# A delta-rule attention and hash-routed experts kernel: TensorE products placed by a count of work, and the first three groups loaded by 192 KB

## The chip, the core and the metric

The kernel runs on one core of one Trainium2 chip. The metric is the device time of one launch in microseconds (us). The five engines are named as in the profile: PE is TensorE, ACT is ScalarE, DVE is VectorE, POOL is GpSimd, SP is SyncE. PE's clock has two levels, 2.4 GHz (granted clock 1.00) and 1.2 GHz (0.50); the profile's rows give the granted clock of a stretch. PE writes its products to eight banks of PSUM, and ACT and DVE copy them from there.

## What is computed

Stage one is a delta rule over 4 batches, 8 heads, 768 positions and a head size of 48; stage two sends each of the 3072 rows through one of eight experts, which a hash of its token chooses.

```python
for t in range(768):
    y[:, :, t] = einsum('bhd,bhde->bhe', q[:, :, t], state)
    v_old = einsum('bhde,bhd->bhe', state, k_n[:, :, t])      # k_n = k / |k|
    state = state + beta_t * einsum('bhd,bhe->bhde', k_n[:, :, t], v[:, :, t] - v_old)
x = y.transpose(0, 2, 1, 3).reshape(3072, 384)
expert = token_ids * 2654435761 % 8
for e in range(8):
    out[expert == e] = maximum(x[expert == e] @ w1[e], 0) @ w2[e]
```

All arithmetic is in f32.

## The kernel before

Stage one cuts the sequence into 24 chunks of 32 positions. Four chunks form a group, so there are six groups.

For each group, work that doesn't depend on the state goes ahead of the chunks:

- K, Q and V come by 48 KB loads on SP's queue, four for each chunk and tensor (`load`, line 400). A load puts the 32 positions of one batch on 32 partitions, in runs of 192 bytes.
- `turn` (line 433) transposes the four 128x128 blocks of a chunk's K or Q on PE, and ACT copies the result to a tile KQ.
- `gram` (line 460) makes the products of keys with keys and of keys with queries, 128 small ones for two chunks (K and Q together), and ACT copies them to GK and GQ. `first_grams` (line 496) does it for the keys of group 0.
- `inverse` runs on DVE. It transposes GK to NT (line 547), works out scales, and then takes 31 steps, each a multiplication (line 582) and a subtraction (line 580) that need the one before. `turn_back` (line 594) transposes the result to TU. Two inverses can be under way at a time, since their tiles exist twice.

Each chunk then has a chain, in which every step needs the one before: `ask` (line 617, keys with the state, to psX), a subtraction on DVE (line 640, to R), `solve` (line 650, to psX; it needs the tile Tz, which ACT makes of TU), a copy on ACT (line 668, to W), `update` (line 677, to psS) and the copies to the next state (lines 701 and 699). The answers (line 721) and the queries' `ask` fill psY, ACT copies that to x_sb, and POOL scatters it to x_scratch (line 733).

No engine picks its own order. Each piece is a `task` with an estimated duration, and `order()` plays the whole stage with these estimates, engine by engine, and always takes the ready task with the longest way to the end. The instructions are then issued in the order that this play gives, and each engine runs its own in that order.

`order()` also places products whose result nobody reads, `unread` (line 602): a 128x128 identity against up to 512 columns. Before the first `update` they fill planned idle time of PE, with their target in a spare bank. After it, `chunk` itself adds one task with four blocks of 128 columns (`REST`; two blocks from chunk 20 on) behind each `update`, and drops it where a transposition or gram is ready. The play knows one speed of PE.

Stage two begins when the last rows have been scattered. It fetches an expert's rows (`fetch`, xr), transposes them on DVE, and runs two matrix products for each expert (lines 1103 and 1133), with the scatter of the results on POOL. The change doesn't touch it.

## Time and profile before

| | us |
|---|---|
| median of 3 runs (532.03 to 533.23) | 532.6 |
| the profiled execution | 535.72 |
| its span, first to last instruction | 534.1 |

| engine | busy us | share of the span |
|---|---|---|
| PE | 472.0 | 88% |
| DVE | 249.5 | 47% |
| ACT | 159.5 | 30% |
| POOL | 136.7 | 26% |

The shares are means over two stages that differ. The profile's slices show DVE nearly full for the first half of the span and nearly idle later, while PE is full in the second half. The slices also give PE's clock: it is below full in most of the slices of the first half, and full in the second. The chain that ended last, as the page prints it, holds only the last microsecond (a scatter on POOL), so the stages have to be read from rows of stretches.

### The profile page before, as it was taken

What the parts mean: (1) busy time and instruction counts of PE and PEld (TensorE: products, weight loads), DVE (VectorE), ACT (ScalarE), POOL (GpSimd) and SP (SyncE); (2) the same over time, 40 slices, a digit from 0 to 9 for tenths busy, and PEclk for the clock granted to TensorE, in tenths of its full rate; (3) what the DMA queues carried; (4) which work ended last, traced back from release to release, by engine and by line L of the source; (5) the groups of instructions that cost most, each with busy time, mean ns of one, the idle gap of its engine ahead of it and who ended that gap; (6) DMA issues with size and microseconds to landing.
All of it is one profiled execution on the core that took longest, in us unless ns stands there. A gap on an engine that the chain in (4) does not pass through costs nothing. (4 is left out here: it accounts for less than half of the span.)

```text
span 534.1 us, 15767 instructions
## 1 busy us (share of the span) xinstructions
PE 472.0 (88%) x6640; PEld 330.8 (62%) x6640; DVE 249.5 (47%) x735; ACT 159.5 (30%) x339; POOL 136.7 (26%) x166
## 2 busy tenths in 40 slices
PE   7787967898999997988199999999999999999991
PEld 5555655677677765766146657666675766767650
DVE  6584787867978989897022113121121212112100
ACT  2325655556856855664000010000101000010100
POOL 5000000302312112111100171452706244260731
PEclk9759979668969978999789999999999999999997
DMA  4455454546543312252696550905417072000101
GB/s 86 76 88 88 82 88 86 111 103 156 105 83 67 75 49 50 58 203 106 111 306 241 134 191 9 301 29 159 166 35 276 16 227 98 7 35 1 39 18 28
DMA packets 108280, 55.93 MB, mean 105 GB/s; under 512 B 95620, under 2 KB 104269, under 8 KB 107312
## 3 DMA queue, kind: packets, MB, share of 16 engines
q1 hardware_dynamic: 102688, 45.15, 34.9%
q0 software_dynamic: 5472, 9.65, 5.1%
q8 instruction: 53, 0.87, 0.7%
q14 instruction: 19, 0.16, 0.1%
q10 hardware_dynamic: 48, 0.10, 0.0%
HBM read 44.51 MB, written 10.62 MB: 103 GB/s over the span
## 5 line engine op out<-in xcount | busy, mean ns | idle before, releaser
L1103 PE MATMUL h_ps<-xT,w_sb 128*128 128x424 f32 (+3 forms) x384 | 128.8, 495 | 12.1 <-DMA xr<-x_scratch 12.1
L1140 POOL DMA_INDIRECT out_dram<-o_sb,idx x90 | 88.3, 981 | 161.3 <-DVE o_sb L1135 89.6
L1103 PEld LDWEIGHTS h_ps<-xT,w_sb 128*128 128x128 f32 x384 | 73.5, 192 | 65.3 <-issue 28.1
L1133 PE MATMUL o_ps<-h_sb,w_sb 128*128 128x424 f32 (+3 forms) x336 | 112.3, 494 | 0.0
L1133 PEld LDWEIGHTS o_ps<-h_sb,w_sb 128*128 128x128 f32 x336 | 84.4, 251 | 27.2 <-issue 0.3
L1106 ACT ACTIVATE h_sb<-h_ps 128x424 f32<-128x424 f32 (+3 forms) x32 | 15.9, 497 | 232.7 <-PE h_ps L1103 211.2
L1108 DVE TENSOR_SCALAR h_sb<-h_ps 128x424 f32<-128x424 f32 (+3 forms) x32 | 18.1, 565 | 112.5 <-PE h_ps L1103 89.7
L733 POOL DMA_INDIRECT x_scratch<-x_sb,slot x24 | 24.6, 1026 | 160.9 <-ACT x_sb L727 59.6
L580 DVE TENSOR_TENSOR U<-U,tmp 128x31 f32<-128x31 f32 (+15 forms) x186 | 61.3, 338 | 2.4
L582 DVE TENSOR_TENSOR tmp<-U,NT 128x175 f32<-128x175 f32 (+15 forms) x186 | 60.7, 336 | 2.5
L1135 DVE STREAM_TRANSPOSE o_sb<-o_ps 128x384 f32<-128x384 f32 (+2 forms) x21 | 15.6, 743 | 79.4 <-PE o_ps L1133 79.4
L701 ACT ACTIVATE S<-psS 48x384 f32<-48x384 f32 x86 | 41.8, 486 | 13.6 <-PE psS L677 8.8
L650 PE MATMUL psX<-R,Tz 64*64 64x48 f32 x736 | 32.3, 235 | 10.1 <-DVE R L640 8.3
L650 PEld LDWEIGHTS psX<-R,Tz 64*64 64x64 f32 x736 | 27.5, 147 | 16.5 <-DVE R L640 8.1
L721 PE MATMUL psY<-W,MT 64*64 64x48 f32 x768 | 33.7, 234 | 1.6 <-issue 1.6
L677 PE MATMUL psS<-W,K 32*128 32x96 f32 x736 | 32.1, 310 | 1.1 <-issue 0.8
L531 ACT ACTIVATE Tz<-TU,kmask 128x256 f32<-128x256 f32 x48 | 31.1, 728 | 0.9 <-DVE TU L594 0.7
L677 PEld LDWEIGHTS psS<-W,K 32*128 32x128 f32 x736 | 27.4, 209 | 4.6 <-ACT W L668 1.7
L617 PE MATMUL psX<-S,KQ 128*32 128x96 f32 x736 | 27.5, 275 | 3.0 <-ACT S L701 2.0
L617 PE MATMUL psY<-S,KQ 128*32 128x96 f32 x736 | 26.6, 277 | 3.3 <-ACT x_sb L727 2.1
L721 PEld LDWEIGHTS psY<-W,MT 64*64 64x64 f32 x768 | 28.6, 147 | 1.3 <-issue 1.1
L617 PEld LDWEIGHTS psY<-S,KQ 128*32 128x32 f32 x736 | 18.9, 124 | 12.1 <-ACT S L701 5.3
(144 smaller groups left out, 475.9 us busy)
## 6 DMA issues: line engine op xcount, KB each, us to landing
w_sb<-in_moe_w_dram SPq DMA_DIRECT2D x14, 1536.0 KB
K<-in_k_dram SPq DMA_DIRECT2D x96, 48.0 KB
Q<-in_q_dram SPq DMA_DIRECT2D x96, 48.0 KB
V<-in_v_dram SPq DMA_DIRECT2D x96, 48.0 KB
xr<-x_scratch SPq DMA_DIRECT2D x16, 145.5 KB
w_sb<-in_moe_w_dram SPq DMA_DIRECT2D x3, 512.0 KB
w_sb<-in_moe_w_dram SPq DMA_DIRECT2D x4, 384.0 KB
out_dram<-o_sb,idx POOLq DMA_INDIRECT x90
```

The source lines that it names most:

```text
L531: lambda e=e: nc.scalar.activation(out[:, :, :, e], in_, ACT.Copy, scale=kmask[:, e:e + 1]))
L580: nc.vector.tensor_tensor(U[:, n:, 0:n], U[:, n:, 0:n], t, op=ALU.subtract)
L582: nc.vector.tensor_tensor(t, U[:, j:n, 0:n].to_broadcast([P, m, n]), NT[:, j, n:, None].to_broadcast([P, m, n]), op=ALU.mult)
L617: nc.tensor.matmul(res[quarter(to), u], lhsT=KQ[:, u, a, quarter(b)], rhs=S0[:, b, u].rearrange("p r d -> p (r d)"), start=(fresh and u == ...
L650: nc.tensor.matmul(pws[i][rows, h], lhsT=Tz[rows, h].rearrange("p e i -> p (e i)"), rhs=R[rows, h], start=(h == hs.start), stop=True, skip ...
L677: nc.tensor.matmul(psS["all"][:, b, 2 * D * u:2 * D * u + 2 * D], lhsT=K[quarter(b), u].rearrange("p r d -> p (r d)"), rhs=W[quarter(b), 2 ...
L701: nc.scalar.activation(to, new, ACT.Copy)
L721: nc.tensor.matmul(py[to, h], lhsT=MT[rows, h].rearrange("p e i -> p (e i)"), rhs=W[rows, h], start=(c == 0 and h == 0), stop=True, skip_g ...
L733: put = nc.gpsimd.indirect_dma_start(out=x_dram[:, :], out_offset=bass.IndirectOffsetOnAxis(ap=slot[:, c:c + 1], axis=0), in_=x_sb.rearran ...
L1103: nc.tensor.matmul(h_ps[:, :width], lhsT=w1_sb[:, co, fo * P:(fo + 1) * P], rhs=xT[:, co, :width], start=(co == 0), stop=(co == CO - 1))
L1133: nc.tensor.matmul(os_ps[i][:, 0:width], lhsT=w2_sb[:, fo, i::CO], rhs=h_sb[:, fo, 0:width], start=(fo == 0), stop=(fo == FO - 1))
L1140: scat = nc.gpsimd.indirect_dma_start(out=out_q, out_offset=bass.IndirectOffsetOnAxis(ap=idx[e][:, k:k + 1], axis=0), in_=o_sb[:, k], in_o ...
```

## The change

1. The first three groups (0 to 2) get their K and Q by 192 KB loads, one for each batch, group and tensor: 128 positions on 128 partitions (`load_batches`). `turn_batches` transposes them, and the results go to three new tiles KQg that hold a group each. The 192 KB loads borrow the last four K tiles. `load` stays for the other groups, for V, and for the K that `update` reads. All K and Q of groups 0 to 2 are listed ahead of chunk 0, with all grams of groups 1 and 2.
2. `order()` now counts the work in PE's array. A task has an `area`, and `run` adds it up by spans of the constant `WINDOW` from a fixed start (`PHASE`). In the span after one with too little (`SHARE`) the play runs PE at half speed.
3. Products are placed by this play everywhere, not by `chunk`. They go into planned idle time, and where the sum lately is below `FORCE`, a whole one is placed even if nothing is idle. After the first `update` the target is psX0, the bank z0, or psS; to psS goes a product with zeros (`add_nothing`), which adds nothing to the state. `REST` and its task are gone.
4. The groups' priorities (`HASTE`), and the estimates of a load's issue and rate, are new numbers.

```diff
-        NK, NQ, NV, NKQ = 7, 2, 3, 14
-        HASTE, DRAG = 10000.0, 1.0
+        NK, NQ, NV, NKQ, NEAR = 7, 2, 3, 14, 3
+        TURNS = [(0, 0), (1, 0), (0, 1), (1, 1), (2, 0), (2, 1)]
+        HASTE = {(0, 3): 25000.0, (0, 4): 25000.0, (0, 5): 25000.0}
...
-        FILL_NS, AFTER, REST, EARLY = 215, 200, 4, 34
+        FILL_NS, AFTER, EARLY = 215, 200, 34
+        PHASE, WINDOW, SHARE, FORCE = 1200.0, 3413.33, 0.36, 0.40
...
+        KQgs = tiles(NEAR, "KQg", [P, GC, HU, 2, P])
+        KQs = [t[:, i] for t in KQgs for i in range(GC)]
+        KQs += tiles(NKQ - len(KQs), "KQ", [P, HU, 2, P])
...
+            def speed(w):
+                full = PHASE + w * WINDOW < 9000 or work.get(w - 1, 0.0) >= SHARE * WINDOW
+                return 1.0 if full else 0.5
...
+            def lately(t):
+
+                return sum(a * (e - max(b, t - WINDOW)) / (e - b) for b, e, a in runs[-24:]
+                           if e > t - WINDOW)
...
+                if e == "PE":
+
+                    idle = until
+                    while idle > 6000:
+                        k = speed(int((idle - PHASE) // WINDOW))
+                        m = min(BANK // P, int((s - AFTER - idle) * k // FILL_NS))
+                        if begun_state and lately(s) < FORCE * WINDOW:
+                            m = BANK // P
+                        z = banks[0] is not None and banks[0] <= idle
+                        to = 0 if not begun_state else 1 if open_x else 2 if z else 3 if (
+                            open_s is not None and open_s <= idle) else None
+                        if m < (1 if not begun_state else 2) or to is None:
+                            break
+                        m = min(m, 3) if to == 3 else m
+                        fills.append((idle + 1, -(m + 8 * to)))
+                        idle = run(idle, FILL_NS * m, 214.0 * m)
...
-                    while idle + FILL_NS + AFTER <= s and idle > 6000 and not begun_state:
-                        k = min(BANK // P, int((s - AFTER - idle) // FILL_NS))
-                        fills.append((idle + 1, -k))
...
+        def load_batches(g, a):
+            for b in range(B):
+                t, names = by_batch(g, a, b)
+                task("SP", 450, (), names, lambda t=t, b=b: nc.sync.dma_start(
+                    out=t.rearrange("p u r d -> p (u r) d")[:, :, 0:D],
+                    in_=(k_r, q_r)[a][b][GC * C * g:GC * C * g + GC * C]), kb=192)
...
+        def add_nothing(n):
+
+            nc.tensor.matmul(psS["all"][:, 0, 0:n * P].rearrange("p (x y) -> p x y", y=P),
+                             lhsT=nought, rhs=ident[:, None, :].to_broadcast([P, n, P]),
+                             start=False, stop=True, skip_group_check=True)
...
-                n = REST if c < SHARED else REST // 2
-                task("PE", 264 * n, ("psS",), ("psX0",),
-                     lambda: unread(psXs[0], n), words=4, kind="U", filler=True)
...
-            for p in range(4):
-                load_k(p)
-            for c in range(GC):
-                turn(c, 0)
+            load_batches(0, 0)
+            load_batches(1, 0)
+            turn_batches(0, 0)
...
+            load_batches(0, 1)
+            turn_batches(1, 0)
+            load_batches(1, 1)
+            turn_batches(0, 1)
             gram(range(GC), (1,))
+            load_batches(2, 0)
+            turn_batches(1, 1)
+            load_batches(2, 1)
...
```

What this moves is shown at three places. In the rows a matmul's target stands ahead of the arrow and its operands behind, with rows x columns; x8 is a count.

SP at the program's start, before:

```order
L400 DMA K0_75<-in_k_dram 32x8x48 x8
L400 DMA K1_76<-in_k_dram 32x8x48 x8
L400 DMA Q0_82<-in_q_dram 32x8x48 x4
L400 DMA Q1_83<-in_q_dram 32x8x48 x4
L400 DMA Q0_82<-in_q_dram 32x8x48 x4
```

and now (Q0 and Q1 are 48 KB loads for chunks 12 to 15):

```order
L460 DMA K3_78<-in_k_dram 128x8x48 x2
L460 DMA K4_79<-in_k_dram 128x8x48 x2
L460 DMA K5_80<-in_k_dram 128x8x48 x2
L460 DMA K6_81<-in_k_dram 128x8x48 x2
L447 DMA Q0_82<-in_q_dram 32x8x48 x6
L460 DMA K5_80<-in_q_dram 128x8x48
L447 DMA Q0_82<-in_q_dram 32x8x48
```

Sixteen 48 KB loads of the first keys became four of 192 KB, the keys of group 1 follow at once, and their queries come before those of group 0. Ahead of the last 192 KB load there are now 23 others and 24 loads of 48 KB.

PE from the last grams ahead of chunk 0 to chunk 1's first `ask`, before:

```order
L602 MATMUL spare3_150<-ident_59 128x512 x3
L602 MATMUL spare3_150<-ident_59 128x384
L650 MATMUL psX0_141<-V0_86,Tz0_116 64x48 x8
L650 MATMUL psX1_142<-V0_86,Tz0_116 64x48 x8
L677 MATMUL psS_1224<-W0_90,K0_75 128x96 x16
L433 MATMUL z0_140<-ident_59,K6_81 128x128 x4
L617 MATMUL psX0_141<-S1_85,KQ1_95 32x96 x8
```

and now:

```order
L689 MATMUL spare3_141<-ident_59 128x512 x2
L689 MATMUL spare3_141<-ident_59 128x384
L743 MATMUL psX0_132<-V0_86,Tz0_107 64x48 x8
L743 MATMUL psX1_133<-V0_86,Tz0_107 64x48 x8
L689 MATMUL spare3_141<-ident_59 128x512 x2
L689 MATMUL spare3_141<-ident_59 128x256
L770 MATMUL psS_1205<-W0_90,K0_75 128x96 x16
L689 MATMUL psX0_132<-ident_59 128x512
L710 MATMUL psX0_132<-S1_85,KQg0_94 32x96 x8
```

The transposition of K6 (a chunk of group 3) no longer stands ahead of chunk 1's `ask`; it comes behind chunk 3's `solve`. Products stand there instead. The transposition of K0 for chunk 14 now stands between the halves of chunk 1's `update`.

PE behind the `update` of chunk 15, before:

```order
L677 MATMUL psS_1224<-W1_91,K0_75 128x96 x16
L602 MATMUL psX0_141<-ident_59 128x512
L617 MATMUL psY_143<-S1_85,KQ1_95 32x96 x8
L617 MATMUL psX0_141<-S0_84,KQ2_96 32x96 x8
L617 MATMUL psY_143<-S1_85,KQ1_95 32x96 x8
L617 MATMUL psX1_142<-S0_84,KQ2_96 32x96 x8
```

and now:

```order
L770 MATMUL psS_1205<-W1_91,K0_75 128x96 x16
L710 MATMUL psY_134<-S1_85,KQg0_94 32x96 x16
L689 MATMUL z0_131<-ident_59 128x256
L710 MATMUL psX0_132<-S0_84,KQg0_94 32x96 x8
L689 MATMUL z0_131<-ident_59 128x256
L710 MATMUL psX1_133<-S0_84,KQg0_94 32x96 x8
```

One product of 512 columns became two of 256, and the queries' `ask` stands ahead of them. From chunk 1 on, the change has 49 blocks of 128 columns of unread products and 16 of zeros; before there were 58 blocks: a product of 512 columns ahead of the `ask` of chunks 4, 8 to 10 and 12 to 20, and one of 256 at chunks 21 to 23. Now chunks 5, 6, 8, 9, 10, 21 and 22 have none at all.

## Rows read from the trace of the kernel before

**Rows 1.** By stretch (start:end, length): busy us, instructions, PEclk, DMA share, GB/s

```profile
core 0: us, PE busy (x) PEld busy (x) DVE busy (x) ACT busy (x) POOL busy (x), PEclk, DMA share, GB/s
...
61.20:98.90 37.70, 29.45 (x664) 22.60 (x658) 29.19 (x102) 21.83 (x48) 2.47 (x4) 0.84 0.48 83
98.90:137.00 38.10, 34.06 (x833) 26.23 (x830) 28.80 (x104) 23.21 (x51) 8.06 (x13) 0.76 0.57 124
137.00:173.00 36.00, 33.64 (x947) 25.99 (x949) 30.57 (x96) 24.44 (x55) 7.22 (x10) 0.86 0.43 85
173.00:206.40 33.40, 30.68 (x975) 23.52 (x964) 29.75 (x92) 21.71 (x49) 6.50 (x10) 0.90 0.28 67
206.40:232.20 25.80, 22.53 (x632) 16.77 (x632) 22.77 (x70) 16.88 (x36) 5.40 (x8) 0.87 0.17 46
...
267.90:534.10 266.20, 254.25 (x768) 166.81 (x768) 48.04 (x85) 16.85 (x34) 93.31 (x93) 0.98 0.37 116
```

**Rows 2.** Timeline of DVE, 38 to 48 us: start, length, names, idle before

```profile
38.27 0.42 DVE L580 TENSOR_TENSOR U<-U,tmp 128x247 f32<-128x247 f32 x1
47.10 1.25 DVE L547 STREAM_TRANSPOSE NT<-GK 128x1024 f32<-128x1024 f32 x1 [8.42 <-ACT GK L471]
```

**Rows 3.** Timeline of SP's queue at the start: start, length, loads issued

```profile
0.94 7.83 SPq L400 DMA_DIRECT2D K<-in_k_dram  x16
8.82 9.88 SPq L400 DMA_DIRECT2D Q<-in_q_dram  x16
```

**Rows 4.** A stretch of 48 KB loads, columns as in rows 1

```profile
18.70:61.00 42.30, 34.83 (x832) 24.28 (x818) 31.09 (x106) 16.43 (x35) 0.00 (x0) 0.80 0.52 87
```

**Rows 5.** A stretch of the expert rows' loads (388-byte runs), columns as before

```profile
262.00:264.00 2.00, 0.00 (x0) 0.00 (x0) 0.00 (x0) 0.00 (x0) 0.00 (x0) 0.50 1.26 217
```

**Rows 6.** Timeline of PE at chunk 0

```profile
64.67 1.14 PE L650 MATMUL psX<-V,Tz 64*64 64x48 f32 x32
```

**Rows 7.** Timeline of PE behind chunk 0

```profile
65.77 1.17 PE L677 MATMUL psS<-W,K 32*128 32x96 f32 x32
70.67 1.09 PE L433 MATMUL z<-ident,K 128*128 128x128 f32 x4 [3.73 <-DMA K<-in_k_dram]
```

**Rows 8.** One stretch at the full clock, two at the lower, columns as before

```profile
90.00:93.40 3.40, 0.93 (x48) 0.81 (x51) 3.40 (x15) 0.65 (x2) 0.00 (x0) 0.99 0.56 100
93.40:103.60 10.20, 10.00 (x226) 7.43 (x217) 8.15 (x29) 5.25 (x11) 3.85 (x5) 0.50 0.53 115
107.00:117.30 10.30, 10.30 (x245) 8.72 (x248) 6.11 (x18) 5.87 (x14) 0.00 (x0) 0.50 0.51 100
```

**Rows 9.** Chunks 10, 12, 14, 17 and 18, update to update, columns as before

```profile
154.50:164.20 9.70, 9.70 (x233) 7.41 (x232) 5.96 (x22) 4.42 (x11) 0.00 (x0) 0.63 0.20 34
171.30:178.25 6.95, 6.48 (x179) 5.00 (x182) 6.67 (x17) 6.75 (x16) 2.18 (x3) 1.00 0.58 118
188.40:197.30 8.90, 8.90 (x227) 7.16 (x227) 6.87 (x24) 3.93 (x10) 0.00 (x0) 0.62 0.18 43
212.40:219.10 6.70, 6.70 (x163) 4.82 (x163) 4.44 (x12) 4.08 (x9) 1.35 (x2) 0.71 0.18 49
219.10:224.70 5.60, 5.13 (x164) 3.77 (x163) 5.39 (x15) 3.95 (x9) 1.19 (x2) 1.00 0.26 66
```

**Rows 10.** Groups of PE: line, names, shapes, count, busy us, mean ns

```profile
L602 PE MATMUL psX<-ident 128*128 128x512 f32 (+1 forms) x32 | 20.2, 712 | 0.4 <-issue 0.4
L460 PE MATMUL z<-KQ 48*32 48x64 f32 x768 | 19.8, 265 | 1.3 <-issue 1.2
...
L433 PE MATMUL z<-ident,K 128*128 128x128 f32 x60 | 10.6, 304 | 3.9 <-DMA K<-in_k_dram 3.7
```

More of the change, by code (lines that the diff above doesn't have):

```diff
@@ L257, in order @@
                 t = tasks[i]
-                rest[i] = t["ns"] * t["drag"] + max([t["more"]] + [lag(i, j) + rest[j] for j in after[i]])
+                rest[i] = t["ns"] + max([t["more"]] + [lag(i, j) + rest[j] for j in after[i]])
             chance = random.Random(SEED)
-            rest = [x + t["boost"] + chance.uniform(-SPREAD, SPREAD)
+            rest = [x + t["boost"] + HASTE.get(t["group"], 0.0) + chance.uniform(-SPREAD, SPREAD)
                     for x, t in zip(rest, tasks)]
@@ L321, in order @@
                 t = tasks[pick]
-                if t["filler"] and any(x <= at + 150 and tasks[i]["kind"] in "GT"
-                                       for x, i in r):
-                    t.update(ns=0, words=0, kind=kind, emit=lambda: None)
                 ready[e] = [p for p in ready[e] if p[1] != pick]
@@ L444, in keys_of @@
         def keys_of(c, parts=(0,)):
-            return tuple(f"KQ{c % NKQ}{a}" for a in parts)
+            return tuple(f"KQ{c % NKQ}{a}{b}" for a in parts for b in range(B))
         def gram(cs, parts=(0, 1)):
@@ L451, in gram @@
             cc, a0, a1 = slice(cs[0] % GC, cs[0] % GC + len(cs)), parts[0], parts[-1] + 1
+            held_keys = [x for c in cs for x in keys_of(c, sorted({0, *parts}))]
             def view(job):
@@ L951, in note @@
             turn_back(0)
[L952 to L958 removed]
+            load_batches(0, 1)
+            turn_batches(1, 0)
+            load_batches(1, 1)
+            turn_batches(0, 1)
+            gram(range(GC), (1,))
+            load_batches(2, 0)
+            turn_batches(1, 1)
+            load_batches(2, 1)
+            for c in range(GC, 2 * GC, 2):
+                gram((c, c + 1))
+            inverse(1)
+            turn_batches(2, 0)
+            turn_batches(2, 1)
+            for c in range(2 * GC, 3 * GC, 2):
+                gram((c, c + 1))
+            turn_back(1)
+            inverse(2)
+            for p in range(NV):
+                load_k(p)
+                load_v(p)
+            for p in range(NV, NK):
+                load_k(p)
             def prepare(p):
                 cs = range(2 * p, 2 * p + 2)
[L963 to L964 removed]
+                group[0] = (0, p // 2)
+                if p >= NK:
                     load_k(p)
```

129 lines of the change are left out of this document (81 added, 48 removed).

## Prediction

> **What bounds the kernel now.** I read the rows by stretch first. Stage two, from 267.9 us to the end, has PE busy 254.25 of 266.20 us at a clock of 0.98 [rows 1]. The change leaves it alone, so whatever is gained must move its start. Up to there a chain of 24 chunks runs beside six inverses on DVE. From the first TU (61.2) to the last (232.2), DVE is busy 29.19 + 28.80 + 30.57 + 29.75 + 22.77 = 141.1 of 171.0 us [rows 1]. Its work there stays, so these 171 us can give at most the 29.9 us in which DVE idles. PE is no less loaded, but part of its load is its own slowness: from the granted clocks, (1 - PEclk) x 2 x length sums to 12.1 + 18.3 + 10.1 + 6.7 + 6.7 = 53.9 us at the lower clock in the same five stretches [rows 1].
>
> Ahead of the chunks, DVE stood 8.42 us in the middle of the first inverse, because the transposition of group 1's GK is next in its order and GK was not there [rows 2]. Behind chunk 0, PE stood 3.73 us for the keys of K6, with chunk 1's `ask` queued behind [rows 7].
>
> **The change, part by part.** The sum is made against the profiled execution, 535.72 us, which is 3.1 above the median of 532.6; I carry the difference over to the median.
>
> *Loads, term a.* SP needed 7.83 us to issue sixteen 48 KB loads, 0.49 each [rows 3], and the loads move 87 GB/s at a DMA share of 0.52 [rows 4]: the issue sets the pace, not the transfer. Now 24 x 192 + 24 x 48 KB = 5.90 MB have to come up to the last large load. If the engines could be filled, 87 / 0.52 = 167 GB/s, they take 35 us. The nearest row with larger loads of short runs is that of the expert rows, 217 GB/s in runs of 388 bytes [rows 5]; at the same number of runs, 192 bytes give 107 GB/s and 55 us. Behind the last load PE still has two transposed batches and group 2's grams before the first `solve`: 16 records at 10.6 / 60 and 256 at 19.8 / 768 us, 9.4 us, plus 21 blocks of products at 20.2 / 58, 7.3 us, where they find no idle time [rows 10]; I take 12. So the first `solve`, now at 64.67 [rows 6], would come at 68 us with 107 GB/s, and at 49 with 167. The other claimant is DVE: group 1's K and Q now come before group 0's Q, and its grams stand before all of group 0's and group 2's, so the 8.42 us should go, and the `solve` can't come before about 64.67 - 8.42 = 56.25. To allow that, the loads need about 137 GB/s, the middle of the two rates. Term a lies between +3.4 and -8.4; I take **-7.5**, a little less than all, as SP also waits for borrowed K tiles to be transposed.
>
> The Trainium skill (DMA: Bandwidth & Descriptors, Bandwidth) gives 138 GB/s already for a 64 KB load, by which term a would be the whole -8.4; its section on small descriptors speaks against this, since the runs stay at 192 bytes. No row here has a 192 KB load of such runs.
>
> *Order behind chunk 0, term b.* K6's transposition goes behind chunk 3's `solve`; its 3.73 us go [rows 7]. In its stead K0's stands between the halves of chunk 1's `update`, and its load can only be issued after chunk 0's `update` and then behind others on SP. Queued behind it are the second half and all that needs the new state. It can give back between nothing and all: 0 to -3.7, taken as **-2.5**.
>
> *Clock, term c.* What a microsecond at the lower clock costs is read from chunks: chunk 14 has 0.76 x 8.90 = 6.8 us of it and takes 1.95 us more than chunk 12, which has none; chunk 10 has 7.2 and takes 2.75 more; chunk 17 has 3.9 and takes 1.10 more than chunk 18 [rows 9]. That is 0.29, 0.38 and 0.28 us for each us; I take 0.32. All 53.9 us would give 17.2. The lower clock came after stretches in which PE stood still: 0.93 us busy of 3.40 up to 93.4 [rows 8]. But it stayed low while PE was busy 10.30 of 10.30 us, from 107.0 on [rows 8]. The new order puts whole-array products into the standstills and spreads group 3's small grams (three blocks of 32 stood in chunk 4, two do now). Yet chunks 14 and 17 had 512 columns of products behind every `update`, and the clock was low there all the same, and the last three chunks lose theirs. So I let a third remain: 36 x 0.32 = **-11.5**, between 0 and -17.2.
>
> *Products, term d.* There are 65 blocks where 58 stood, at 0.35 us each [rows 10]; nearly all fill waits, as those did. The ones placed by force at chunks 7, 11 and 12, between two parts of the chain, wait for DVE's 0.35 us subtraction anyway. I take **+1.5**, between 0 and +4; if nothing covered them, 65 x 0.35 = 22.8 us would be paid.
>
> *Work on ACT, DVE and POOL* is the same in number but for the 24 batch copies in place of 24 chunk copies, so it costs nothing. The extra 2.4 MB of keys are in term a.
>
> Sum: -7.5 - 2.5 - 11.5 + 1.5 = -20.0. That is 515.7 for the profiled execution and **512.6 us** for the median. Of DVE's 29.9 idle us, terms b to d use 12.5.
>
> **The rivals.** *1, the clock is not moved.* PE's clock answers to something that products in gaps below a microsecond don't change; chunks 14 and 17 speak for it, the stretches after standstills against. Then -7.5 - 2.5 + 1.5 = -8.5, 524.1 us. The Trainium skill (TensorE: Matmul & The Clock Gate, Loop structure matters more than you think) has this rule: matmuls that follow back to back stay fast, and long waits make them slow; by it short gaps need no filling. The trace agrees at 90.0, not from 107.0 on.
>
> *2, all of the clock comes back.* Then a and b are whole too, since the play would fit the chip: with d at nothing -8.4 - 3.7 - 17.2 = -29.3, 503.3 us. DVE's 29.9 us allow it (20.9 used). Every wait that DVE would have to lose speaks against it.
>
> *3, slower: the loads stay as slow as now.* PE runs in order, so all of group 2's grams, and the last large load with them, stand before the first `solve`. At the 87 GB/s of now [rows 4], 5.90 MB take 67.8 us, the `solve` comes at 80.8, and a is +16.1 instead of -7.5: +3.6 in all, 536.2 us. The whole turns slower below about 92 GB/s. For it: the runs are no longer than before. Against: a DMA share of 0.52 and the 107 GB/s worked out from rows 5.
>
> *4, the change doesn't do what it says*: the play's estimates drift from the chip, products stand where there is work and miss the standstills. That ends near rival 1, and is counted with it.
>
> **How the numbers follow.** Forecast 0.62 (508 to 518); rival 1 (with 4) 0.15; rival 2 0.14; rival 3 0.06; something else 0.03. The range takes in the forecast and rivals 1 and 2 and reaches from 503 to 524.5; that leaves out the far halves of these two and rival 3, about 2 in 10. A measurement of this kernel can tell about 0.2%, 1.1 us, from no change. Rivals 1 and 2 are faster too, so faster has 0.91, the same 0.02, slower 0.07.
>
> **What would show it.** Right: DVE has no wait of several us for GK before the first TU, and the first `solve` starts near 57 us (term a); the loads' stretch shows well over 107 GB/s. PE's wait for K6 is gone and no other one of over 1.2 us for a K load follows (b). The stretch from the first to the last TU has a granted clock of 0.93 or more, where it was 0.84 to 0.76 in its first half (c). The first product of stage two begins near 248 instead of 267.9. Wrong: the clock is as before with more products (rival 1); the first `solve` waits for transposed K3 or K4 (rival 3); or DVE idles as long as now with the clock up, so that another wait, of the chain on ACT or SP, has taken the place of the clock.

## The result and the profile after

| | before | changed |
|---|---|---|
| median, us (lowest to highest) | 532.32 (529.91 to 533.23) | 524.18 (523.47 to 526.70) |
| the profiled execution, its span | 535.72, 534.1 | 523.64, 522.0 |
| first solve starts | 64.67 | 59.37 |
| chunk 0's update ends | 66.94 | 64.15 |
| first TU, last TU (from rows 1) | 61.2, 232.2 | 52.8, 212.5 |
| chunk 22's update ends | 248.47 | 235.78 |
| first product of stage two | 267.9 | 255.0 |

The ratio is 0.9863 with a 95% interval of 0.9815 to 0.991: the medians lie 8.1 us apart, where 20 were forecast. The medians of e5 and e13 further down each take in one execution far above the others (1513.91 and 608.43 us), which the ratios leave out. The time lies just inside the range (503 to 524.5), and it is that of rival 1, "the clock is not moved". But the clock did move. The rows below are stretches of the changed kernel from TU to TU and stage two, as in [rows 1]: length, busy us (instructions) of PE, PEld, DVE, ACT and POOL, granted clock, DMA share, GB/s.

```profile
core 0: us, PE busy (x) PEld busy (x) DVE busy (x) ACT busy (x) POOL busy (x), PEclk, DMA share, GB/s
52.80:89.90 37.10, 31.69 (x773) 21.35 (x774) 27.35 (x95) 20.07 (x46) 0.95 (x1) 0.91 0.47 82
89.90:123.00 33.10, 29.64 (x871) 22.61 (x865) 30.03 (x108) 24.34 (x53) 9.01 (x13) 0.95 0.56 117
123.00:156.70 33.70, 28.58 (x900) 21.49 (x892) 28.18 (x95) 23.21 (x51) 5.93 (x9) 0.95 0.53 102
156.70:186.90 30.20, 24.15 (x787) 17.99 (x784) 28.64 (x95) 19.17 (x43) 5.89 (x9) 1.00 0.42 95
186.90:212.50 25.60, 24.47 (x712) 18.07 (x716) 21.66 (x60) 18.88 (x41) 6.35 (x10) 0.93 0.29 76
255.00:522.00 267.00, 255.15 (x768) 167.26 (x768) 47.99 (x85) 16.85 (x34) 93.05 (x93) 0.97 0.37 115
```

The clock is 0.91 to 1.00 where it was 0.76 to 0.90, and each stretch up to the last TU is shorter, 159.7 us in all where 171.0 stood. DVE idles for 23.8 us instead of 29.9. Stage two is as before. The last TU comes 19.7 us sooner, which is nearly the whole forecast; but the last update comes only 12.7 us sooner, because the chain of chunks now ends 23.3 us behind the last TU, where it ended 16.3 behind. And the first update, ahead of which term a put 7.5 us, gained 2.8.

On DVE the start went as forecast. The second NT has no wait any more, where [rows 2] show 8.42 us. Start, length, line, names:

```profile
36.38 0.42 DVE L668 TENSOR_TENSOR tmp<-U,NT 128x255 f32<-128x255 f32 x1
36.73 1.24 DVE L633 STREAM_TRANSPOSE NT<-GK 128x1024 f32<-128x1024 f32 x1
```

The new first TU ends at 52.8, 8.4 us sooner. What follows it on ACT and PE is where term a fell short. First ACT, then PE, from the last grams of group 2 to the first update:

```profile
54.33 0.64 ACT L555 ACTIVATE GK<-psY 128x256 f32<-128x256 f32 x1 [3.20 <-PE psY L544]
54.76 1.53 ACT L555 ACTIVATE GK<-spare 128x256 f32<-128x256 f32 x3
56.08 0.42 ACT L555 ACTIVATE GQ<-psY 128x256 f32<-128x256 f32 x1
56.38 2.25 ACT L616 ACTIVATE Tz<-TU,kmask 128x256 f32<-128x256 f32 x4
...
61.82 0.70 ACT L555 ACTIVATE GQ<-spare 128x256 f32<-128x256 f32 x2
```

```profile
57.24 2.20 PE L689 MATMUL spare<-ident 128*128 128x512 f32 x5 [1.27 <-issue]
59.37 1.14 PE L743 MATMUL psX<-V,Tz 64*64 64x48 f32 x32
60.44 2.42 PE L689 MATMUL spare<-ident 128*128 128x512 f32 x6
63.00 1.15 PE L770 MATMUL psS<-W,K 32*128 32x96 f32 x32
```

TU is there at 52.8, but ACT takes its copies in order, and group 2's GK stand ahead of Tz. So Tz comes at 58.63, and the solve at 59.37. The update then starts at 63.00. Both waits are looked at again below (e5, e13).

The loads show why group 2's grams are so late. Two stretches, and SP's issues of 192 KB loads (first 8, last 4):

```profile
0.00:18.10 18.10, 14.07 (x350) 10.66 (x350) 10.22 (x32) 4.96 (x7) 7.97 (x21) 1.00 0.98 124
18.10:52.80 34.70, 29.82 (x759) 22.35 (x759) 31.51 (x109) 16.07 (x34) 0.00 (x0) 0.95 0.73 125
```

```profile
0.94 8.15 SPq L460 DMA_DIRECT2D K<-in_k_dram  x8
...
40.98 5.01 SPq L460 DMA_DIRECT2D K<-in_k_dram  x4
```

The loads moved 125 GB/s instead of 87, and an issue took 8.15 / 8 = 1.02 us where a 48 KB load took 0.49 [rows 3]. The last keys of group 2 were issued from 41 to 46 us.

### The profile page after: what moved, and what is told of

It reads as the page before. It is cut to its first block, busy times and chain, and to the rows that moved or that the text cites. A ratio compares the mean times of both kernels' runs of the same rounds, so it can differ in the third digit from the quotient of the medians.

```text
span 522.0 us, 15767 instructions
## 1 busy us (share of the span) xinstructions
PE 463.1 (89%) x6670; PEld 321.7 (62%) x6670; DVE 245.0 (47%) x735; ACT 159.1 (30%) x339; POOL 136.1 (26%) x166
## 5 line engine op out<-in xcount | busy, mean ns | idle before, releaser
L1240 POOL DMA_INDIRECT out_dram<-o_sb,idx x90 | 88.0, 978 | 162.3 <-DVE o_sb L1235 89.9
L668 DVE TENSOR_TENSOR tmp<-U,NT 128x31 f32<-128x31 f32 (+15 forms) x186 | 59.1, 335 | 1.5
L666 DVE TENSOR_TENSOR U<-U,tmp 128x31 f32<-128x31 f32 (+15 forms) x186 | 58.8, 335 | 1.4
L743 PEld LDWEIGHTS psX<-R,Tz 64*64 64x64 f32 x736 | 26.4, 142 | 12.7 <-DVE R L733 5.9
L616 ACT ACTIVATE Tz<-TU,kmask 128x256 f32<-128x256 f32 x48 | 33.5, 741 | 1.2 <-ACT KQg L520 0.5
L810 PE MATMUL psY<-W,MT 64*64 64x48 f32 x768 | 32.4, 229 | 0.1
L710 PE MATMUL psX<-S,KQg 128*32 128x96 f32 x672 | 24.6, 266 | 7.1 <-ACT S L790 3.9
L770 PE MATMUL psS<-W,K 32*128 32x96 f32 x736 | 29.1, 290 | 0.4 <-issue 0.2
L810 PEld LDWEIGHTS psY<-W,MT 64*64 64x64 f32 x768 | 27.3, 142 | 0.4 <-issue 0.3
L631 POOL MEMSET U<- 128x1024 f32 x6 | 5.7, 954 | 81.9 <-DVE TU L681 42.9
L770 PEld LDWEIGHTS psS<-W,K 32*128 32x128 f32 x736 | 24.3, 191 | 4.0 <-issue 1.4
L710 PEld LDWEIGHTS psX<-S,KQg 128*32 128x32 f32 x672 | 15.0, 114 | 17.6 <-ACT S L790 8.3
```

What stands on the lines that cost most here:

```text
L616: lambda e=e: nc.scalar.activation(out[:, :, :, e], in_, ACT.Copy, scale=kmask[:, e:e + 1]))
L666: nc.vector.tensor_tensor(U[:, n:, 0:n], U[:, n:, 0:n], t, op=ALU.subtract)
L668: nc.vector.tensor_tensor(t, U[:, j:n, 0:n].to_broadcast([P, m, n]), NT[:, j, n:, None].to_broadcast([P, m, n]), op=ALU.mult)
L710: nc.tensor.matmul(res[quarter(to), u], lhsT=KQ[:, u, a, quarter(b)], rhs=S0[:, b, u].rearrange("p r d -> p (r d)"), start=(fresh and u == ...
L743: nc.tensor.matmul(pws[i][rows, h], lhsT=Tz[rows, h].rearrange("p e i -> p (e i)"), rhs=R[rows, h], start=(h == hs.start), stop=True, skip ...
L770: nc.tensor.matmul(psS["all"][:, b, 2 * D * u:2 * D * u + 2 * D], lhsT=K[quarter(b), u].rearrange("p r d -> p (r d)"), rhs=W[quarter(b), 2 ...
```

## The experiments

All times are medians; each ratio is to the kernel before, run beside it on the same chip. Runs from different chips are compared by the ratios. "Chunks" is the stretch from the end of chunk 0's update to the end of chunk 22's in the profiled execution, with its granted clock.

| run | us | ratio (interval) | chunk 0's update ends | chunks, us | clock |
|---|---|---|---|---|---|
| before | 532.32 | 1 | 66.94 | 181.5 | 0.85 |
| changed | 524.18 | 0.9863 (0.9815 to 0.991) | 64.15 | 171.6 | 0.93 |
| e15, changed again | 524.45 | 0.9886 (0.9838 to 0.9933) | 63.80 | 171.4 | 0.92 |
| e1, none behind the first update | 526.79 | 0.986 (0.9807 to 0.9913) | 65.43 | 172.8 | 0.87 |
| e5, none from 41 us to it | 525.06 | 0.9858 (0.9816 to 0.99) | 65.07 | 170.3 | 0.94 |
| e9, both | 523.01 | 0.9874 (0.9828 to 0.992) | 65.43 | 170.3 | 0.86 |
| e13, idle ones only | 521.55 | 0.9798 (0.9748 to 0.9848) | 64.09 | 172.4 | 0.87 |
| e11, before without products | 529.08 | 0.9939 (0.9905 to 0.9973) | 67.31 | 171.9 | 0.85 |
| e4, products alone | 544.6 | 1.022 (1.0176 to 1.0264) | 74.42 | 183.3 | 0.93 |
| e3, loads and priority alone | 528.06 | 0.9885 (0.9843 to 0.9928) | 66.59 | 175.8 | 0.90 |
| e8, loads alone | 523.47 | 0.9889 (0.9845 to 0.9934) | 63.58 | 172.4 | 0.88 |
| e14, loads, no products behind | 522.19 | 0.9828 (0.978 to 0.9876) | 63.87 | 173.0 | 0.86 |
| e7, priority alone | 545.92 | 1.0307 (1.0265 to 1.035) | 77.96 | 179.8 | 0.89 |
| e10, small loads | 544.62 | 1.0261 (1.0221 to 1.03) | 64.25 | 193.5 | 0.92 |
| e6, Q later | 527.44 | 0.994 (0.9903 to 0.9976) | 62.30 | 179.9 | 0.91 |
| e18, four V tiles | 522.35 | 0.979 (0.9733 to 0.9847) | 65.48 | 171.0 | 0.83 |
| e19, four V tiles, V first | 525.02 | 0.9873 (0.9817 to 0.9929) | 61.70 | 176.3 | 0.81 |

**Are the products worth anything?** The theory was that the clock makes most of the gain. In six kernels (e1, e5, e9, e11, e13 and e14) products are left out where the order is issued, so that every other instruction keeps its place.

e1, no product behind the first update:

```diff
                     n, to = -i % 8, -i // 8
+                    if to > 0:
+                        continue
```

> The changed kernel without the 65 blocks of products behind the first update; every other instruction keeps its place. Theory (the clock is what the products buy, terms c and d of the prediction): the time at the lower clock between chunk 0 and chunk 22 goes from 24 us to 50 or more, which at 0.32 us each costs 8, and the products' own 1.5 us are saved: about 531 us. Rival 1 (the clock answers to something else, the lower clock went for another reason, such as the new order of grams and loads): 24 us as now and 522 to 524 us. A third case, that the products cost on the chain about what the clock gives back: clock lower, but the time within 2 us of the 524.2 of the changed kernel.

e5, the 40 blocks from 41 us to the first update left out:

```diff
+                    early += to == 0
+                    if to == 0 and early > 10:
+                        continue
```

> The changed kernel without the 40 blocks of products that stand from 41 us to the first update (the pile of 9 blocks at 41 us, those among group 2's transpositions and grams, and those around the first solve); all other instructions keep their place. Theory (term a fell short because PE was late, not the loads or DVE): the first update ends at 59 to 61 us instead of 64.15, and the time falls by 3 to 5 us, to 520 us. Rival A (the loads or TU set it): first update at 64, time 524. Rival B (without these products PE goes to the lower clock in group 2's grams and loses there what it saves): first update at 63 to 66 with a granted clock near 0.5 from 48 to 60 us.

e9, both (`if to > 0 or early > 10`):

> The changed kernel without any product from 41 us on, before and behind the first update (e1_none_behind and e5_none_late_in_start together); every other instruction keeps its place. It measures the price of the lower clock at one order of work: theory, 60 to 80 us at the lower clock up to the last update, and a price of 0.1 to 0.15 us each, as between the changed kernel and e1_none_behind: 526 to 529 us. Rival (0.32 us each, as the prediction had it): 533 us or more.

The chunks of the kernel before, of the changed kernel, of e1 and of e9:

```profile
66.94:248.47 181.53, 157.36 (x4387) 121.70 (x4387) 152.24 (x491) 112.88 (x246) 30.94 (x45) 0.85 0.42 97
```

```profile
64.15:235.78 171.63, 148.21 (x4398) 111.12 (x4402) 143.05 (x477) 112.00 (x242) 30.73 (x46) 0.93 0.47 106
```

```profile
65.43:238.22 172.79, 137.44 (x4348) 111.50 (x4352) 142.54 (x476) 112.19 (x242) 31.17 (x46) 0.87 0.46 105
```

```profile
65.43:235.68 170.25, 140.31 (x4348) 112.80 (x4352) 143.06 (x477) 112.19 (x242) 32.14 (x47) 0.86 0.46 106
```

By (1 - PEclk) x 2 x length the lower clock takes 24, 45 and 48 us of the last three, so the products do raise the clock. These chunks take 171.6, 172.8 and 170.3 us: twice the time at the lower clock, and no time lost. The whole kernel has the ratio 0.9863, 0.986 and 0.9874. So e1's third case is what happened. e9's rival, 533 us or more, fell, and so did its theory, 526 to 529, on the other side (523.01). This refutes a price of 0.32 us together with products that cost little; it does not tell the price from the products' cost.

That doesn't make the lower clock free. I cut the chunks of the two pairs (changed and e1, e5 and e9) from update to update and fitted the difference of each of the 44 chunks by the difference in time at the lower clock and by the products' own time. A us at the lower clock costs 0.19 us (standard error 0.06), a us of products 0.23 (0.10). The 26.8 us of products in the changed kernel's chunks then cost 6 and give back 4. The two other pairs that differ by products alone (before and e11, e8 and e14) give 0.61 (0.11) and 0.26 (0.11) by the same fit, and all four pairs together 0.29 (0.05) and 0.30 (0.08): a cost of 8 and a return of 6. The pairs don't agree on the price of the clock; in both fits the products cost more than they return. These are estimates from one profiled execution of each kernel.

e11 does the same to the kernel before (its 58 blocks become no instruction):

```diff
-                     lambda: unread(psXs[0], n), words=4, kind="U", filler=True)
+                     lambda: None, words=4, kind="U", filler=True)
```

> The kernel before without the 58 blocks of products behind its updates; every other instruction keeps its place. Theory (in these chunks the lower clock costs about what the products cost, so that neither old nor new products bring anything): the lower clock in the chunks rises from 54.6 us to 65 or more and the time stays within 2 us of the kernel before. Rival (term c's price of 0.32 us holds, products cost little): 4 us or more above the kernel before.

```profile
67.31:239.24 171.93, 139.18 (x4360) 114.44 (x4364) 151.85 (x491) 113.22 (x246) 31.30 (x45) 0.85 0.44 102
```

The clock is 0.85 with and without these blocks (51 us at the lower clock, not 65), and by the ratio the time is 0.6% less without them (0.0061 x 531 = 3.2 us, interval 1.4 to 5.0). The old products cost more than they gave, which neither expectation held. With 48 KB loads, these chunks take 171.9 us, as few as those of the changed kernel.

e4 puts the new rule of products into the kernel before (with one rule of the changed kernel that its plan needs: a gram waits for the keys of both its chunks):

> The kernel before with its 48 KB loads, its order of groups and its estimates, and with the new count of the array's work and the new placing of products in place of the old. Theory: the start is as before (first solve near 64.7 us), the lower clock in the chunks falls from 54 us to under 30, and the time falls by 0.32 us for each of these less what products on the chain cost: 524 to 528 us. Rival (the products only pay together with the order that the new loads give): clock as before, 532 to 536 us.

Clock 0.93 as in the changed kernel, time 2.2% more. The plan was made anew with the slower PE that it now reckons with, and put other work late: the first solve starts at 68.22, the first update ends at 74.42, and chunk 4 alone takes 29.6 us. Here the plan's order outweighs anything that the clock gives.

e13 keeps only the products for planned idle time behind the first update, and none between the first solve and the first update:

```diff
-                        if begun_state and lately(s) < FORCE * WINDOW:
+                        forced = begun_state and lately(s) < FORCE * WINDOW and m < BANK // P
+                        if forced:
                             m = BANK // P
...
+                    if forced or (solved and to == 0):
+                        continue
```

> The changed kernel without the five products behind the first update that were placed by force (17 blocks, in chunks 2, 3, 7, 11 and 12 or their neighbours) and without the ten blocks between the first solve and the first update; all else keeps its place. Theory (term d was sized too small: these stand on the chain, the ten blocks 2 us ahead of the first update): the first update ends near 62 us, chunks 7 and 11 are 1 to 2 us shorter each, the time at the lower clock rises by no more than 10 us, and the time is 520.5 to 522.5 us. Rival (what they cost the clock gives back): 523.5 to 525 us.

By the ratio the time is 0.7% below the changed kernel's, about where the theory had it, but the intervals overlap. The theory's reason is not seen: the first update ends at 64.09 as in the changed kernel, the lower clock takes 45 us of the chunks where the theory allowed 34, and the chunks are no shorter in the profiled execution (523.88; others go down to 518.07). What made those shorter was not seen.

**What holds the first update?** Without products in the way PE still waits. e5 on PE, the last keys' transpositions, the first solve and the first update:

```profile
47.45 0.63 PE L474 MATMUL psX<-ident,K 128*128 128x128 f32 x4 [0.43 <-DMA K<-in_k_dram]
48.53 0.63 PE L474 MATMUL z<-ident,K 128*128 128x128 f32 x4 [0.45 <-DMA K<-in_k_dram]
49.67 0.63 PE L474 MATMUL psX<-ident,K 128*128 128x128 f32 x4 [0.51 <-DMA K<-in_k_dram]
...
59.06 1.95 PE L743 MATMUL psX<-V,Tz 64*64 64x48 f32 x32 [2.03 <-ACT Tz L616]
63.04 2.04 PE L770 MATMUL psS<-W,K 32*128 32x96 f32 x32 [2.03 <-ACT GQ L555]
```

e5's theory fell: the products had only filled waits. They are for the loads of group 2's keys, then for Tz behind ACT's copies of group 2's GK, and then for its copies of GQ out of the spare banks, which the update's psS takes over. Rival B's lower clock came too, here from 52 to 68 us, and cost 0.9 us:

```profile
52.00:68.00 16.00, 10.80 (x283) 8.20 (x266) 9.01 (x22) 8.98 (x20) 0.95 (x1) 0.50 0.40 72
```

e6 lets the 48 KB loads of Q, which stand on SP ahead of these keys, be planned only from 40 us on:

```diff
-                         hold=16000 * (x == "v"))
+                         hold=16000 * (x == "v") + 40000 * (x == "q"))
```

> The changed kernel, where the 48 KB loads of Q (groups 3 to 5) may not be planned before 40 us: in the changed kernel sixteen of them stand on SP's queue ahead of group 2's keys. The plan is made anew by this, products included. Theory (term a fell short since the last large loads land late; at 125 GB/s instead of 137 the prediction's own sum gives a first solve at 60): the first solve comes at 54 to 57 us instead of 59.4, the first update ends at 57 to 60 instead of 64.15, and 3 us or more of this reach the end: 519 to 522 us. Rival A (PE's own work and its issue gaps hold the first solve): first solve at 58 to 60, time 524. Rival B (the start is earlier, but the inverses on DVE hold the chunks): first update 4 us earlier and the time within 1.5 us of 524.

SP's issues of group 2's keys in e6, which started at 40.98 in the changed kernel, and e6's first 20 us:

```profile
25.28 2.98 SPq L460 DMA_DIRECT2D K<-in_k_dram  x3
...
29.30 0.65 SPq L460 DMA_DIRECT2D K<-in_k_dram  x1
```

```profile
0.00:20.00 20.00, 15.31 (x353) 11.72 (x354) 10.42 (x33) 5.01 (x7) 7.96 (x21) 0.90 1.09 142
```

These keys were no longer late, yet the first solve was still at 59.13, as rival A had it: in this plan the first TU came at 56.8 instead of 52.8, and ACT made Tz from 57.83 on. The first update came 1.9 us sooner, but the chunks took 8.3 us more: the second TU came at 86.2 (89.9 in the changed kernel), the third at 126.1 (123.0), and chunk 4 took 22.0 us. For the end it is rival B's outcome with more given back than it allowed.

**Is it the loads or the order?** e3 has the changed kernel's loads and priorities and the old rule of products; e8 has the old priority as well; e14 drops e8's products behind updates (58 blocks by e8's trace, 54 of them behind chunk 1 and later). e7 has the new priority in the kernel before, with the rule on grams that e4 has too. The edit by which e8 differs from e3:

```diff
-        HASTE = {(0, 3): 25000.0, (0, 4): 25000.0, (0, 5): 25000.0}
+        HASTE = {(0, 3): 10000.0, (0, 4): 10000.0, (0, 5): 10000.0}
```

> The changed kernel's loads, transpositions and priorities with the old rule of products: one of 512 columns behind each update, dropped where a transposition or gram is ready, and a play with one speed. Theory: the loads are worth what the start showed, 3 us, and the order behind chunk 0 some 2 us, with the clock of before (about 50 us of lower clock in the chunks): 527 to 529 us. Rival, the loads and the order make all the gain: 524 us with the clock up at 0.95. Rival, the loads alone give nothing, because the products set where PE is late: 532 us.

> The run e3_loads_alone with the priority of the work of groups 3 to 5 at the 10000 of the kernel before: so large loads, old priority, old rule of products. Theory (priority makes the gain in chunks 12 to 22): these chunks take 75 us or more, 7 more than in e3_loads_alone, and the time is 531 to 534 us. Rival (the loads make it, since the groups' work starts sooner whatever the priority): 527 to 529 us as in e3_loads_alone.

> The run e8_loads_old_haste (large loads, old priority, old rule of products) without its 54 blocks of products behind the updates; every other instruction keeps its place. Theory (products behind an update cost about what the clock gives back or more, as e11_before_no_products showed with a gain of 2 to 3 us): 519 to 522 us, with 45 us or more at the lower clock in the chunks. Rival (they pay for themselves): 523 to 525 us.

> The kernel before with the priority of the work of groups 2 to 5 at 25000 instead of 10000, and with a gram that waits for the keys of both its chunks, as in the changed kernel; loads and the rule of products as before. In its plan the grams of group 5 end at chunk 11, where the kernel before has them at chunks 12 to 14. Theory (the chunks became shorter because group 4's and 5's transpositions and grams come earlier, not because of the products): chunks 12 to 22 take 68 to 71 us together instead of 77, and the time is 525 to 529 us. Rival (the early work is only moved into chunks 1 to 11 and costs there what it saves later): 531 to 534 us.

The chunks of e8 and of e14:

```profile
63.58:236.00 172.42, 148.16 (x4375) 113.20 (x4375) 146.10 (x479) 110.90 (x242) 34.33 (x45) 0.88 0.46 105
```

```profile
63.87:236.87 173.00, 133.93 (x4349) 109.74 (x4352) 145.69 (x479) 110.97 (x242) 34.20 (x45) 0.86 0.45 105
```

e8 has the changed kernel's whole gain (0.9889; the changed kernel 0.9863 and 0.9886) with neither its products nor its priority, and e14 as much or more. So the loads, with the order of groups that goes with them, are worth about 5.9 us with the old products (e8 against before, interval 3.5 to 8.2) and as much with none (e14 against e11, 0.9828 / 0.9939 = 0.9888, about 2.8 to 9.0). Of this, 3.4 us stand ahead of the end of the first update in both pairs (66.94 to 63.58, 67.31 to 63.87). In the chunks the profiled executions of the two pairs disagree: 181.5 to 172.4 with the old products, 171.9 to 173.0 with none.

The new priority makes no difference that a run can tell: e3 has 0.9885, e8 0.9889, against e8's theory of the total. It moves time between chunks: chunks 12 to 22 take 68.1 us in e3 and 77.2 in e8, as that theory had it, and chunks 1 to 11 take 107.7 and 95.2. In e7, too, chunks 12 to 22 became shorter (63.6 us, before 77.2), and chunks 1 to 11 longer (116.2, before 104.4). There the plan also put group 1's grams behind other work; DVE waited 13.55 us for them, the first update ended at 77.96, and the time rose by 3%:

```profile
63.62 1.25 DVE L548 STREAM_TRANSPOSE NT<-GK 128x1024 f32<-128x1024 f32 x1 [13.55 <-ACT GK L472]
```

e10 keeps everything else and issues each 192 KB load as four of 48 KB:

```diff
-                task("SP", 450, (), names, lambda t=t, b=b: nc.sync.dma_start(
-                    out=t.rearrange("p u r d -> p (u r) d")[:, :, 0:D],
-                    in_=(k_r, q_r)[a][b][GC * C * g:GC * C * g + GC * C]), kb=192)
+                for i in range(GC):
+                    c = GC * g + i
+                    task("SP", 490, (), names[i:i + 1], lambda t=t, b=b, i=i, c=c: nc.sync.dma_start(
+                        out=t.rearrange("p u r d -> p (u r) d")[quarter(i), :, 0:D],
+                        in_=(k_r, q_r)[a][b][C * c:C * c + C]), kb=48)
```

> The changed kernel with each 192 KB load of groups 0 to 2 issued as four of 48 KB into the same tile; the order of groups, the borrowed tiles, the batch transpositions and the rule of products stay (the plan is made anew). Theory (the size of the loads makes the gain, since SP's issue sets their pace): 96 issues at 0.49 us where the changed kernel has 24 at about 1.02; at 0.49 us for 48 KB, 98 GB/s, the prediction's 5.90 MB take 60 us and the first solve comes near 73 us, 14 later than in the changed kernel; two thirds of that or more reach the end: 533 to 538 us. Rival (the new order of groups makes the gain, not the size): first solve at 59 to 62 us and 524 to 527 us.

The price was higher than expected, 2.6% above the kernel before, and in another place. The plan, made anew, put group 2's grams behind chunk 0, so the first solve came at 60.0. Then chunk 1 took 19.7 us. DVE's third and fourth NT of the changed kernel, and of e10, show what the pace of the loads does to the inverses:

```profile
62.99 1.24 DVE L633 STREAM_TRANSPOSE NT<-GK 128x1024 f32<-128x1024 f32 x1
102.10 1.24 DVE L633 STREAM_TRANSPOSE NT<-GK 128x1024 f32<-128x1024 f32 x1
```

```profile
84.07 1.25 DVE L635 STREAM_TRANSPOSE NT<-GK 128x1024 f32<-128x1024 f32 x1
121.81 1.24 DVE L635 STREAM_TRANSPOSE NT<-GK 128x1024 f32<-128x1024 f32 x1
```

In the kernel before they start at 75.29 and 112.24; in e10 21 and 20 us later than in the changed kernel. From 20 to 60 us e10 moves 88 GB/s, as the kernel before in [rows 4]:

```profile
20.00:60.00 40.00, 34.44 (x625) 22.39 (x623) 32.42 (x113) 14.12 (x29) 0.95 (x1) 0.87 0.51 88
```

So the new order of groups is a loss with small loads, and the gain needs the large ones, which bring the groups' inverses forward. How much of the 21 us between e10 and the changed kernel is the size itself and how much the plan made anew is not told apart.

**What holds the chunks now?** e15 is the changed kernel beside e14 on one chip. e14 lies 0.6% below it, but the intervals overlap. Against e9 (0.9874) e15 has 0.9886, 0.6 us apart, as the theory had it.

> The changed kernel itself, beside e14_loads_no_products on one chip, as the measure for it and for the runs with other products. Theory: 522 to 526 us, within 1.5 us of e9_none_from_41 against their kernels before, so that all products from 41 us on are worth no more than that. Rival (the products do pay): 2 us or more below e9_none_from_41 by the ratios.

e14 shows two waits for V on DVE:

```profile
148.33 0.56 DVE L613 TENSOR_TENSOR V<-V,ntok 128x384 f32<-128x384 f32 x1 [6.61 <-DMA V<-in_v_dram]
...
182.57 0.56 DVE L613 TENSOR_TENSOR V<-V,ntok 128x384 f32<-128x384 f32 x1 [6.56 <-DMA V<-in_v_dram]
```

e18 adds a fourth V tile (`NV` 4 instead of 3), and e19 also puts the loads of V ahead (`boost=20000 * (x == "v" and p >= 3)`):

> The run e14_loads_no_products with four tiles for V instead of three; the plan is made anew. In e14_loads_no_products DVE waited 6.6 us twice for a load of V (chunks 10 and 13). Theory (with the start and the inverses no longer late, waits for loads on SP's queue are what is left, and they reach the end): the two waits shrink to under 3 us each, and the time falls by half of what they lose or more: 515 to 520 us. Rival A (V comes no sooner, since its loads stand behind K and Q on SP): 522 us. Rival B (the waits go, but the chain of the last chunks takes the gain back): the waits gone and 521 to 523 us.

> As e18_four_v, and the loads of V from chunk 6 on have a priority of 20000, so that they stand ahead of more of the loads of K and Q on SP. Theory: both waits for V gone, 514 to 519 us. Rival (K and Q of groups 4 and 5 come later instead, and their inverses with them): 522 to 526 us.

e18 lost the second wait (chunk 13 takes 10.8 us instead of 16.5) and kept the first, 6.50. Its time is 522.35, as e14's, with the best ratio of all, 0.979; whether that is better than e14's 0.9828 can't be told. e19 lost both and brought nothing. Its clock was 0.81 and its chunks 5 us longer than e18's. For e18 that is rival A for the first wait and rival B for the second; for e19 the time is the rival's, though only one of the last two inverses starts later than in e18 (141.2 and 176.3, there 137.1 and 179.7).

## Why the prediction was wrong

The sum was made against the profiled execution: -20.0. That fell by 12.1: 2.8 ahead of the end of the first update, 9.9 in the chunks, 0.2 behind them, and stage two took 0.8 more. The medians differ by only 8.1, and that is the last step: I carried the 3.1 us by which the old profiled execution lay above its median over to the result, but the new one lies 0.5 below its own.

**Term a, -7.5, measured -2.8.** DVE's 8.42 us went as said. One mis-sized step is the rate: "the loads need about 137 GB/s, the middle of the two rates". They got 125. By the prediction's own sum 5.90 MB then take 47.2 us, and with the 12.9 us behind them (68 - 55.1) the first solve comes at 60.1; it came at 59.37. The Trainium skill (DMA: Bandwidth & Descriptors, Bandwidth) has 138 GB/s for a 64 KB load, measured with loads issued from GpSimd; here loads from SP in runs of 192 bytes, of 192 and of 48 KB, moved 125 in the changed kernel, and 142 in the first 20 us of e6, and the measurement decides. The upper end, 167 GB/s, came from dividing 87 by a share of 0.52; at a share of 0.98 the engines moved 124. That the rate alone held the solve is not shown: with group 2's keys 11 us sooner, e6 has it at the same time. The other part is ACT, whose work the prediction put at nothing ("costs nothing"): group 2's copies stand ahead of Tz and ahead of the update, and PE waits some 2 us more for them between the first solve and the update (e5).

**Term b, -2.5.** K6's 3.73 us went and chunk 1 is 2.6 us shorter (7.8 us instead of 10.4). In its stead K0's transposition waited 1.70 us, over the bound of 1.2 that I had set. Here is that row:

```profile
70.67 0.63 PE L514 MATMUL z<-ident,K 128*128 128x128 f32 x4 [1.70 <-DMA K<-in_k_dram]
```

PE's waits for K loads in the chunks are 3.8 us in four pieces instead of 3.7 in one. So the term held in its place and was given back later.

**Term c, -11.5, and term d, +1.5: the step that failed.** The new products and their clock were to bring 10.0 us together. Left out at an unchanged order, they proved to bring nothing that a run can tell (0.9863 with them, 0.986 in e1 and 0.9874 in e9 without). Two sizes of the sum were wrong.

The first is how much of the lower clock the products remove. The total came out: I let a third of 53.9 us remain, 18; by the same working the new stretches have 6.7 + 3.3 + 3.4 + 0 + 3.6 = 17.0. But that was in part luck. With no product behind the first update e1 has 45 us at the lower clock in its chunks, where the kernel before has 54.6, so the products remove 21 us (27 between e9 and e5), not 36.

The second is term d. "Nearly all fill waits" was the assumption. The products filled waits ahead of the first update (e5, e13), but behind it the fits put their cost at 6 to 8 us instead of 1.5, and what they return in clock at 4 to 6 instead of 11.5.

The price, 0.32 us for each us at the lower clock, was read badly but is not shown to be wrong. [rows 9] set chunks side by side that hold different work: chunk 10 has 233 instructions of PE and chunk 14 has 227, where chunk 12 has 179, since the slow chunks also held grams. Only chunks 17 and 18 (163 and 164) compare clock with clock, 0.28. The fits give 0.19 with two pairs and 0.29 with four.

**What the sum did not have.** The loads are worth about 5.9 us by the ratios (e8 against before, e14 against e11), where the sum had them ahead of the first update alone, which gained 2.8 to 3.4. That leaves some 2.5 us for the chunks, an estimate with an interval as wide as itself, and not the 9.9 that lie between the two profiled executions: e11's chunks are as short with 48 KB loads. What the traces do show is that SP was late with what the first chunks need. Freed from this, every inverse behind the first starts 10 us or more sooner, and two waits of DVE for the grams of later groups, in the kernel before, have no counterpart in the changed one:

```profile
112.24 1.25 DVE L547 STREAM_TRANSPOSE NT<-GK 128x1024 f32<-128x1024 f32 x1 [1.60 <-ACT GK L471]
159.10 1.25 DVE L547 STREAM_TRANSPOSE NT<-GK 128x1024 f32<-128x1024 f32 x1 [2.55 <-ACT GK L471]
```

I had the 29.9 us of DVE's idle time as a limit, but didn't ask what it waited for. Not each wait for a load that goes is time gained. Between the first and the second TU the timeline of DVE before had these:

```profile
67.79 0.18 DVE L759 TENSOR_SCALAR rt<-tid 128x32 int32<-128x32 int32 x1 [3.69 <-DMA tid<-in_moe_token_ids_dram]
89.22 0.56 DVE L522 TENSOR_TENSOR V<-V,ntok 128x384 f32<-128x384 f32 x1 [2.94 <-DMA V<-in_v_dram]
```

The changed kernel waits 2.97 us for the tokens in that stretch and for no V in it, but the stretch is only 0.6 us shorter (37.1 instead of 37.7), since DVE waits 6.5 us there for PE's psX.

**The rivals.** Rival 1 had the time, for another reason: the clock moved and was worth nothing net. By the rule of the Trainium skill that stood beside it (TensorE: Matmul & The Clock Gate, Loop structure matters more than you think), as the prediction read it, short gaps need no filling; the time agrees, the clock doesn't, since the products raised it from 0.87 to 0.93 (e1). Of the signs of being wrong, the last comes nearest: the clock is up, and DVE still idles 23.8 of its 29.9 us. Rival 3's condition was good: e10 loads at 88 GB/s, below its 92, and is slower than the kernel before, by 13.7 us where the rival had 3.6, though in the chunks and not ahead of them. Rival 4 wasn't tested apart.

**Left open.** With 192 KB loads the chunks take 170 to 176 us at clocks from 0.81 to 0.94, whatever the order and the products (179.9 in e6), but e11 takes 171.9 with 48 KB loads. So what sets the chunks' time is not shown. In e8 and e14 the last update comes 16.9 us after the last TU, as before (16.3), which speaks for DVE's inverses as what holds the end; in the changed kernel it comes 23.3 us after it, which speaks for the chain. That two bounds lie close together would explain why taking either away alone moved nothing; no run tests it. A third wait, of POOL for a write of zeros, stands in all these traces; it is the last point below.

## What to carry to other kernels

Price a slow clock only between stretches with the same instructions, and test it by leaving the cure out at an unchanged order: here twice the time at the lower clock cost nothing net. If an issuing queue sets the pace of small loads, larger loads can pay beyond the start, in what the queue was late with; ask of each idle gap of the pacing engine what it waits for, and what it would wait for next. Where a planner makes the order, an edit to its costs moves work elsewhere, so change the issued order itself when one cause is to be measured. The profiled executions of two kernels can lie further apart than their medians (here 12.1 and 8.1 us), so take a part of a gain from them only where the medians bear it out.

## What the hardware showed

- A 192 KB load in runs of 192 bytes took SP 1.02 us to issue (eight in 8.15), a 48 KB load 0.49; with the engines at a share of 0.98 they moved 124 GB/s.
- 58 blocks of 512- and 256-column products left the granted clock of the old chunks at 0.85, with and without; the 65 new ones raise it from 0.87 to 0.93.
- In e6, whose first loads are nearly all of 192 KB, the engines moved 142 GB/s at a share of 1.09 over the first 20 us.
- In the changed kernel POOL stood still for 16.34 us although ACT had finished the x_sb tiles to be scattered at 172.97 and 178.31; ACT's next x_sb waited for the scatter, and PE for ACT. POOL's row, then PE's:

```profile
183.38 1.11 POOL L822 DMA_INDIRECT x_scratch<-x_sb,slot  x1 [16.34 <-ACT W L761]
```

```profile
187.03 0.87 PE L710 MATMUL psY<-S,KQg 128*32 128x96 f32 x32 [2.86 <-ACT x_sb L816]
```

The row names an instruction of ACT, but the traces of e1, e5, e6, e8, e10, e13 and e14 name another releaser for the same wait: a write of 700 KB of zeros to the same x_scratch, which SP issues (`clear_pad`, line 1017). SP's row in the changed kernel, then SP's and POOL's in e1:

```profile
177.61 0.73 SPq L1017 DMA_DIRECT2D x_scratch<-zrow  x1
```

```profile
180.90 0.88 SPq L1017 DMA_DIRECT2D x_scratch<-zrow  x1
...
186.67 1.04 POOL L822 DMA_INDIRECT x_scratch<-x_sb,slot  x1 [17.82 <-DMA x_scratch<-zrow]
```

In both kernels the scatter starts 5.8 us after this write was issued, in all 17 traces 5.6 to 6.8 us after it. In the kernel before it was issued at 117.90, and POOL stood still for 16.46 us until 123.46. PE waits for the x_sb behind it up to 4.0 us (e13) and in e8 and e14 not at all. No run moves the write, so what it costs the whole is not shown.
